# Banded attention followed by an MLP mixer: bfloat16 transposes, nine realigned score blocks, direct global columns and a bfloat16 bias pass

## The chip, the cores and the metric

The kernel runs on 1 core of one Trainium2 chip. The metric is the device time of one execution in microseconds (us), as the median of several executions. In this document PE is the TensorE matmul stream, PEld its weight loads, DVE VectorE, ACT ScalarE, POOL GpSimd and SP SyncE. "L306" means line 306 of the kernel that is being profiled, so a line number belongs to one kernel only.

## The reference

There are 8 batches of 8 heads, 576 positions, head size 64. Attention is limited to a band of ±32 positions, except that 8 "global" positions see everything and are seen by everything. Its output is the input of an MLP mixer (token mixing with a 576x576 matrix, then 512 → 2048 → 512 with ReLU).

```python
scores = scale * np.matmul(q, k.transpose(0, 1, 3, 2))      # scale = 1/8
mask = np.abs(pos[:, None] - pos[None, :]) <= 32
mask = mask | is_global[:, None] | is_global[None, :]
attn = softmax(np.where(mask, scores, -1e9))
x = (attn @ v) -> (batch, seq, 512)
a1 = alpha1 * x + beta1;  u = x + lam * einsum('ts,bsd->btd', w_tok, a1)
a2 = alpha2 * u + beta2;  out = u + lam * (np.maximum(a2 @ w_ch1, 0) @ w_ch2)   # float32
```

## The kernel before

There are three stages, and the profile shows them one after the other: setup (masks, weights in bfloat16, a bias vector), 64 attention heads, and the MLP. In these traces each engine runs its own instruction stream in a fixed order; the order within each engine is settled by a scheduler when the kernel is built, from the order in the source, the buffers and the dependences.

The bias pass of setup multiplies the raw float32 weights with `beta2`, one column at a time:

```python
W1[:, cc, :] = w1raw[:, cc, :] * a2c[:, cc]          # DVE, float32 -> bf16, 4 times (cut)
for ec in range(16):
    for cc in range(4):
        nc.tensor.matmul(out=bps[:, ec : ec + 1],
                         lhsT=w1raw[:, cc, ec * P : (ec + 1) * P],   # float32
                         rhs=b2c[:, cc : cc + 1], start=(cc == 0), stop=(cc == 3))
```

One head (cuts marked). `pA` has 2 buffers; the PSUM pools for the scores, the values (`pvps`) and the transposes (`trps`) have 1 each.

```python
BLOCKS = [(t, c) for t in range(5) for c in range(5) if abs(t - c) <= 1]   # 13 blocks

for h in range(H):
    dma_640(qn, qf, bh, nc.sync); dma_640(kn, kf, bh, nc.sync); dma_640(vn, vf, bh, nc.gpsimd)
    nc.scalar.copy(out=vext[:, :, 0:D], in_=vn)                    # ACT, to float16
    trps = psA_tr.tile([64, NT, P], FP32, name="trps")
    for c in range(NT):
        nc.tensor.transpose(out=trps[:, c, :], in_=qn[:, c, :], identity=ident)   # float32
    nc.vector.tensor_copy(out=QT, in_=trps)                        # DVE -> bf16
    for c in range(NT):
        nc.tensor.transpose(out=trps[:, c, :], in_=kn[:, c, :], identity=ident)   # same buffer
    nc.scalar.copy(out=KT, in_=trps)                               # ACT -> bf16

    nc.tensor.transpose(out=pvps[0:8, PV_VG:PV_VG+64], in_=vgT[:, 8*h:8*h+8], identity=...)
    nc.vector.tensor_copy(out=vg_ext[:, 0:D], in_=pvps[0:8, PV_VG:PV_VG+64])

    for bi, (t, c) in enumerate(BLOCKS):
        nc.tensor.matmul(out=scps[:, bi*P:(bi+1)*P], lhsT=KT[:, c, :], rhs=QT[:, t, :], ...)
        # ... where t == c: two products of 8 columns, for the global rows and global columns
    nc.scalar.activation(out=PT, in_=scps, func=AF.Exp, bias=0.0, scale=0.125)    # 1744 columns
    nc.vector.tensor_tensor(out=PT, in0=PT, in1=mask, op=ALU.mult)

    for t in range(NT):       # weights of the global columns, transposed on PE
        nc.tensor.transpose(out=pvps16[0:8, ...], in_=PT[:, GC_OFF+8*t : GC_OFF+8*t+8], identity=ident16)
    nc.vector.tensor_copy(out=pgcT, in_=pvps16[0:8, ...])
    for t in range(NT):       # values
        nc.tensor.matmul(out=pvps[:, t*65:t*65+65], lhsT=pgcT[:, t, :], rhs=vg_ext, ...)
        for c in neighbours(t):   # 13 in all
            nc.tensor.matmul(out=pvps[:, t*65:t*65+65], lhsT=PT[:, bi*P:(bi+1)*P], rhs=vext[:, c, :], ...)
    # ... 5 products for the global rows; then pvps -> xstg (DVE) and pvps -> xg (ACT)
```

The softmax here doesn't subtract the row's maximum and nothing guards it: scores larger than these inputs give would overflow.

## Time and profile before

The median is 1051.45 us (4 runs, 1050.48 to 1051.78). The profiled execution has a span of 1048.0 us. The stages are cut at the first score product and at the last copy into `xstg`:

| stage | us | what fills it |
|---|---|---|
| setup | 0 to 85.2 | DMA of weights, bias pass on PE, W2 on DVE, transposes of `w_tok` |
| 64 heads | 85.2 to 680.3 (595.1, or 9.30 a head) | PE |
| MLP | 680.3 to 1048.0 (367.7) | PE |

The windows view of before gives the busy time of each engine in each stage (in parentheses the number of instructions), then the granted clock, the busy share of the DMA engines and GB/s:

```profile
0.00:85.20 85.20, 41.05 (x177) 33.74 (x177) 28.93 (x86) 2.34 (x4) 7.83 (x14) 1.00 0.43 145
85.20:680.30 595.10, 500.61 (x3978) 324.07 (x3978) 200.82 (x531) 184.62 (x253) 89.03 (x151) 1.00 0.26 68
680.30:1048.00 367.70, 333.60 (x1987) 196.92 (x2024) 127.21 (x154) 127.17 (x257) 1.47 (x1) 1.00 0.17 59
```

The columns after the window's length are PE, PEld, DVE, ACT and POOL. In the heads PE is busy for 500.6 of 595.1 us, 84%; no other compute engine reaches 35%, and DMA stands at 0.26.

The chain of waits on before's page says what the end of the run followed from, here by engine (the page goes on by line):

```profile
PE 76%; DVE 9%; ACT 6%; DMA 5%; issue 2%; POOL 0%; SPq 0%; ACTq 0%; POOLq 0%; DVEq 0%
```

The same chain in order of time, over one head of before. Columns: start in us, duration in us, and what the chain passes through:

```profile
329.92 0.23 PE trps L291
...
330.17 0.83 DVE QT L292
331.00 0.04 issue
331.04 1.29 PE trps L294 x5
...
332.40 0.69 ACT KT L295
333.09 0.05 issue
333.14 0.28 PE scps L306
...
337.52 1.22 PE trps L291 x5
...
338.77 0.83 DVE QT L292
```

This is the pattern to see. There is one transpose buffer. PE transposes q into it (1.22 us), waits for DVE to copy it out (0.83 us), transposes k into it (1.29 us), and can do scores only when ACT has copied KT (0.69 us). From 331.04 to 339.64 (where the next k transposes start) is 8.6 us; many heads are longer, since the static order differs from head to head.

This is the timeline of before (columns: start, duration, engine, line and operation; in brackets the idle time of the engine before it and what ended it):

```profile
332.25 0.69 PE L327 MATMUL pvps<-ident,PT 128*8 128x128 f16 x5
333.14 0.28 PE L306 MATMUL scps<-QT,KT 64*128 64x128 bf16 x1 [0.20 <-ACT KT L295]
```

Over 530 us of heads (110 to 640 us) the two largest of PE's waits in the waits view are these (columns: total us, times, longest):

```profile
PE trps L294 <- DVE QT L292: 35.4, 43, 0.9
PE scps L306 <- ACT KT L295: 19.5, 43, 0.9
```

The groups view of before gives busy time and mean duration (ns) of the instructions that the change touches; after the second bar stands the idle time of the engine ahead of them and what ended it:

```profile
L294 PE MATMUL trps<-ident,kn 128*64 128x128 f32 x320 | 88.1, 421 | 54.3 <-DVE QT L292 38.8
L323 ACT ACTIVATE PT<-scps 128x1744 f16<-128x1744 f32 x64 | 103.9, 1624 | 77.6 <-PE scps L315 76.6
...
L295 ACT CAST KT<-trps 64x640 bf16<-64x640 f32 x64 | 43.8, 685 | 144.1 <-PE trps L294 129.8
...
L292 DVE CAST QT<-trps 64x640 bf16<-64x640 f32 x64 | 52.2, 815 | 53.3 <-PE trps L291 53.3
```

A transpose's record of 421 ns overlaps the next one's: five of them take 1.22 to 1.29 us in the chain, not 2.1.

The setup of before, again the chain in order of time:

```profile
16.56 13.12 DMA w1raw<-in_moe_w_ch_dram
...
29.81 27.45 PE bps L199 x128
...
57.46 9.62 DVE W L184 x16
```

The bias pass (its 64 float32 products stand in the trace as 128 passes, two each) takes 27.45 us on PE, and DVE's work on W2 comes after it.

### The profile page before, as it was taken

To read this page: it belongs to the slowest core of one execution; us is meant where nothing else is said; L and a number is where in the kernel's file an instruction comes from. 1 tells how busy PE (TensorE), PEld (TensorE's weight loads), DVE (VectorE), ACT (ScalarE), POOL (GpSimd) and SP (SyncE) were. 2 spreads that over 40 slices of the span, in tenths; PEclk is the share of its full clock that TensorE was granted. 3 is DMA by queue.
4 is the path that set the end of the run, shared out by engine and by line. 5 is a ranking of instruction groups with operands and counts; after the bars stand their busy time and mean duration, and the time that the engine had idled before them with its cause. 6 is when DMAs were issued, how large, how long until landed. Compare 5 with 4: busy or idle time off the path is not lost.

```text
span 1048.0 us, 14830 instructions
## 1 busy us (share of the span) xinstructions
PE 875.3 (84%) x6142; PEld 554.7 (53%) x6179; DVE 357.0 (34%) x770; ACT 314.1 (30%) x513; POOL 98.3 (9%) x165
## 2 busy tenths in 40 slices
PE   0857888888888888888888888629999999999988
PEld 0835555555555555555545555406565565565654
DVE  3152333333333233333333333345335144143021
ACT  0003233323333332333223333204152361441532
POOL 0004121111121011121111110000000000000000
PEclk9999999999999999999999999999999999999999
DMA  5603223223223132232232232041202112011001
GB/s 172 251 13 87 58 58 103 53 51 109 57 71 90 45 110 58 58 99 50 58 108 58 51 102 49 1 153 51 97 20 78 45 53 97 31 66 46 21 26 46
DMA packets 111291, 74.70 MB, mean 71 GB/s; under 512 B 89080, under 2 KB 89608, under 8 KB 110712
## 3 DMA queue, kind: packets, MB, share of 16 engines
q1 hardware_dynamic: 106088, 62.75, 20.3%
q0 software_dynamic: 5136, 11.00, 3.6%
q8 instruction: 49, 0.80, 0.3%
q14 instruction: 18, 0.15, 0.0%
HBM read 53.51 MB, written 20.22 MB: 70 GB/s over the span
## 4 chain that ended last, share of the span: by engine, by line
PE 76%; DVE 9%; ACT 6%; DMA 5%; issue 2%; POOL 0%; SPq 0%; ACTq 0%; POOLq 0%; DVEq 0%
PE chps L437 13%; PE hps L428 12%; PE scps L306 10%; PE pvps L340 8%; PE trps L294 7%; PE trps L291 7%; PE pvps L337 5%; DVE QT L292 4%; ACT KT L295 4%; PE tkps L403 3%; PE bps L199 3%; PE pvps L327 2%; PE pvps L348 2%; DMA X<-xdram 2%; PE utps L417 1%
## 5 line engine op out<-in xcount | busy, mean ns | idle before, releaser
L431 ACT ACTIVATE HT<-hps,bias1T 128x288 bf16<-128x288 f32 x256 | 127.0, 500 | 222.8 <-PE hps L428 222.8
L437 PE MATMUL chps<-W,HT 128*128 128x512 bf16 (+1 forms) x611 | 151.7, 380 | 0.8 <-issue 0.3
L428 PE MATMUL hps<-UT,W 128*128 128x288 bf16 x1024 | 147.4, 284 | 2.6 <-DVE UT L420 0.6
L306 PE MATMUL scps<-QT,KT 64*128 64x128 bf16 x832 | 123.9, 293 | 22.6 <-ACT KT L295 22.6
L294 PE MATMUL trps<-ident,kn 128*64 128x128 f32 x320 | 88.1, 421 | 54.3 <-DVE QT L292 38.8
L323 ACT ACTIVATE PT<-scps 128x1744 f16<-128x1744 f32 x64 | 103.9, 1624 | 77.6 <-PE scps L315 76.6
L428 PEld LDWEIGHTS <-W 128*128 128x128 bf16 x1024 | 98.9, 97 | 45.4 <-issue 21.2
L357 DVE COPY xstg<-pvps 128x320 f32<-128x320 f32 x64 | 31.4, 491 | 214.2 <-PE pvps L348 214.2
L340 PE MATMUL pvps<-vext,PT 128*128 128x65 f16 x832 | 103.5, 241 | 0.0
L441 DVE TENSOR_TENSOR ob<-chps,U 128x512 f32<-128x512 f32 (+1 forms) x40 | 27.6, 690 | 201.9 <-PE chps L437 175.7
L437 PEld LDWEIGHTS <-HT 128*128 128x128 bf16 (+1 forms) x640 | 62.2, 100 | 63.2 <-issue 3.4
L291 PE MATMUL trps<-ident,qn 128*64 128x128 f32 x320 | 89.7, 420 | 4.7 <-ACT KT L295 4.7
L294 PEld LDWEIGHTS trps<-ident,kn 128*64 128x64 f32 x320 | 42.5, 157 | 91.3 <-DVE QT L292 58.1
L306 PEld LDWEIGHTS <-KT 64*128 64x128 bf16 x832 | 66.3, 113 | 45.7 <-ACT KT L295 36.1
L295 ACT CAST KT<-trps 64x640 bf16<-64x640 f32 x64 | 43.8, 685 | 144.1 <-PE trps L294 129.8
L284 ACT CAST vext<-vn 128x320 f16<-128x320 f32 x64 | 29.3, 458 | 182.3 <-PE pvps L348 182.3
L337 PE MATMUL pvps<-vg_ext,pgcT 8*128 8x65 f16 x320 | 73.7, 230 | 0.6 <-DVE pgcT L333 0.6
L403 PE MATMUL tkps<-XL,wtT 128*128 128x512 bf16 (+2 forms) x192 | 52.0, 390 | 24.5 <-DVE XL L394 22.1
L292 DVE CAST QT<-trps 64x640 bf16<-64x640 f32 x64 | 52.2, 815 | 53.3 <-PE trps L291 53.3
L324 DVE TENSOR_TENSOR PT<-PT,mask 128x1744 f16<-128x1744 f16 x64 | 67.2, 1050 | 3.6 <-ACT PT L323 3.6
L308 PE MATMUL scps<-qgT,KT 64*128 64x8 bf16 x320 | 67.3, 210 | 0.0
L340 PEld LDWEIGHTS <-PT 128*128 128x128 f16 x832 | 52.8, 116 | 20.6
(82 smaller groups left out, 813.4 us busy)
## 6 DMA issues: line engine op xcount, KB each, us to landing
xdram<-xstg SPq DMA_DIRECT2D x8, 1300.0 KB, 6.4
X<-xdram SPq DMA_DIRECT2D x8, 1300.0 KB, 5.9
qn<-in_q_dram SPq DMA_DIRECT2D x63, 160.0 KB, 2.7
kn<-in_k_dram SPq DMA_DIRECT2D x63, 160.0 KB, 2.4
vn<-in_v_dram POOLq DMA_DIRECT2D x63, 160.0 KB, 3.2
out_dram<-ob SPq DMA_DIRECT2D x32, 256.0 KB, 2.0
w1raw<-in_moe_w_ch_dram SPq DMA_DIRECT2D x1, 4096.0 KB, 13.1
w2raw<-in_moe_w_ch_dram SPq DMA_DIRECT2D x1, 4096.0 KB
```

The source lines that it names most:

```text
L291: nc.tensor.transpose(out=trps[:, c, :], in_=qn[:, c, :], identity=ident)
L292: nc.vector.tensor_copy(out=QT, in_=trps)
L294: nc.tensor.transpose(out=trps[:, c, :], in_=kn[:, c, :], identity=ident)
L295: nc.scalar.copy(out=KT, in_=trps)
L306: nc.tensor.matmul(out=scps[:, bi * P : (bi + 1) * P], lhsT=KT[:, c, :], rhs=QT[:, t, :], start=True, stop=True)
L323: nc.scalar.activation(out=PT, in_=scps, func=AF.Exp, bias=0.0, scale=0.125)
L337: nc.tensor.matmul(out=pvps[:, t * PV_T : t * PV_T + PV_T], lhsT=pgcT[:, t, :], rhs=vg_ext, start=True, stop=False)
L340: nc.tensor.matmul(out=pvps[:, t * PV_T : t * PV_T + PV_T], lhsT=PT[:, bi * P : (bi + 1) * P], rhs=vext[:, c, :], start=False, stop=(ci == ...
L403: nc.tensor.matmul(out=tkps[0:tsz, :], lhsT=wtT[0:ssz, sc, t * P : t * P + tsz], rhs=XL[0:ssz, sc, :], start=(sc == 0), stop=(sc == 4),)
L428: nc.tensor.matmul(out=hps, lhsT=W1[:, cc, ec * P : (ec + 1) * P], rhs=UT[:, cc, tsl], start=(cc == 0), stop=(cc == 3))
L431: nc.scalar.activation(out=HT[:, ec, tsl], in_=hps, func=AF.Relu, bias=bias1T[:, ec : ec + 1], scale=1.0)
L437: nc.tensor.matmul(out=chps[0:tsz, :], lhsT=HT[:, ec, t * P : t * P + tsz], rhs=W2[:, ec, :], start=(ec == 0), stop=(ec == 15))
```

## The change

The intent is to shorten every head on PE and to shorten setup:

- q and k are first cast to bfloat16 (qn on DVE, kn on ACT), and the transposes and their PSUM tile are bfloat16. KT is copied by DVE instead of ACT.
- The 13 score blocks of 128x128 become 9. A tile of 128 queries needs only the keys from 32 before to 32 after it, which fit into two blocks of 128 if these start at an odd multiple of 64 (the first tile keeps its blocks at 0 and 128, the last needs only one). That needs a second load of v, shifted by 64 rows (`vo`, `voext`).
- The weights of the global columns are computed with the global keys as the stationary operand, so they come out already transposed: two products into an own PSUM tile `gcps` and an own exp, in place of five 8-column products, five transposes and a copy.
- The global v rows are transposed once a batch, not once a head. `pvps` gets two buffers.
- The bias pass uses the bfloat16 W1, with beta2/alpha2 as the moving operand.

```diff
-BLOCKS = [(t, c) for t in range(NT) for c in range(NT) if abs(t - c) <= 1]
+BLOCKS = [(0, 0), (0, 128), (1, 64), (1, 192), (2, 192), (2, 320), (3, 320), (3, 448), (4, 448)]
 # ... (tables of the mask for the new blocks cut)
+    nc.vector.reciprocal(out=ra2c, in_=a2c)
+    nc.vector.tensor_tensor(out=b2a, in0=b2c, in1=ra2c, op=ALU.mult)      # bf16
-                    lhsT=w1raw[:, cc, ec * P : (ec + 1) * P],
-                    rhs=b2c[:, cc : cc + 1],
+                    lhsT=W1[:, cc, ec * P : (ec + 1) * P],
+                    rhs=b2a[:, cc : cc + 1],
 # ...
-        tc.tile_pool(name="psA_pv", bufs=1, ...) as psA_pv,
+        tc.tile_pool(name="psA_pv", bufs=2, ...) as psA_pv,
+        tc.tile_pool(name="psA_gc", bufs=1, ...) as psA_gc,
 # ... once a batch:
+            for h in range(H):
+                nc.tensor.transpose(out=vgps[:, 64*h : 64*h+64], in_=vgT[:, 8*h : 8*h+8], identity=...)
+            nc.vector.tensor_copy(out=vg_all[:, :, 0:D], in_=vgps...)
 # ... once a head:
+                nc.vector.tensor_copy(out=qn16, in_=qn)
+                nc.scalar.copy(out=kn16, in_=kn)
+                nc.gpsimd.dma_start(out=vo, in_=vf[bh * S + 64 : bh * S + S, :]...)
+                nc.scalar.copy(out=voext[:, :, 0:D], in_=vo)
-                trps = psA_tr.tile([64, NT, P], FP32, name="trps")
+                trps = psA_tr.tile([64, NT, P], BF16, name="trps")
-                    nc.tensor.transpose(out=trps[:, c, :], in_=qn[:, c, :], identity=ident)
+                    nc.tensor.transpose(out=trps[:, c, :], in_=qn16[:, c, :], identity=identb)
-                nc.scalar.copy(out=KT, in_=trps)
+                nc.vector.tensor_copy(out=KT, in_=trps)
-                        # five: lhsT=QT[:, t, :], rhs=kgT[:, 8*h : 8*h+8]
+                nc.tensor.matmul(out=gcps[0:8, PV_GCB:PV_GCB+128], lhsT=kgT[:, 8*h:8*h+8], rhs=QT[:, 4, :], ...)
+                nc.tensor.matmul(out=gcps[0:8, 512:1024], lhsT=kgT[:, 8*h:8*h+8], rhs=QTf[:, 0:512], ...)
+                nc.scalar.activation(out=pgc, in_=gcps[0:8, PV_GCB:1024], func=AF.Exp, ...)
-                # five transposes of PT's global columns, copy to pgcT
```

## The prediction

> **What bounds it now** (chain of waits, timeline). Setup runs to about 84 us; 64 attention heads from 84 to 680 us (first score matmul to last copy into xstg, 9.31 us a head); the MLP takes 368 us. The chain of waits is 76% PE. From 330 to 347 us (two heads) PE issues about 7.7 us a head: float32 transposes of q and k 1.22 and 1.29 (five each), scores 1.9, five transposes of the global-column weights 0.62, the value products 2.47, one vg transpose 0.2. About 1.6 us a head is PE waiting for the two copies out of the one transpose buffer (QT on DVE 0.82, KT on ACT 0.69).
>
> **What the change does, per head.**
> - Float32 transposes become bfloat16. Five 16-bit transposes of PT take 0.69 us start to end in the trace, 0.62 occupied. Saves about 1.3 us of PE.
> - QT reads 16-bit PSUM. The copy of pgcT (640 16-bit elements from PSUM) takes 0.48 us against 0.82 for 640 float32; the Trainium skill, "VectorE: DVE Perf Modes", section "Why PSUM operands drop a tier", gives the same factor. KT moves to DVE, also 0.48.
> - Score blocks 13 to 9, and five 8-column products become two products of 640 columns: about 1.9 to 1.65 us.
> - Five pgcT transposes and the pgcT copy vanish; value products 2.47 to about 2.05 (at 0.06-0.07 us each).
> - Exp 1744 to 1192 columns: 1.62 to 1.16 us (0.85 ns a column in the trace); mask product 1.05 to 0.77.
> - Added: casts of qn (DVE, 0.25, from the W1 cast) and kn (ACT 0.46), voext (ACT 0.40), exp of pgc (ACT 0.7), a second value load (POOL 0.9, 128 KB).
>
> Sums per head: PE 5.0, ACT 3.4, DVE 2.7, POOL 2.0 us; DMA busy share from 0.27 to about 0.57.
>
> **The new loop.** PE's static order in a head is: scores, one global product, q transposes, k transposes, global-column products, value products. With DVE in the order QT, qn cast, mask: scores end at 1.28, q transposes 2.15, QT 2.66, qn cast 2.83, mask 3.5; meanwhile k transposes and the global products end at 3.65; value products end at 5.6. The period is about 5.65 us, perhaps 6 with slips. At each batch border vg_all is copied from the score buffer before the next scores: about 0.9 us, seven times.
>
> Attention: 64 x 5.75 + 6 + filling, about 380 us against 596: 216 saved.
>
> **Setup.** The 128 float32 passes for bias1T (27.4 us on PE, holding DVE) become 64 bfloat16 ones, about 5 us after W1. Then W2 (copied from 57.4 us on) waits for its DMA, done near 42 us by the DMA share in windows. About 15 us saved; DVE's longer mask setup (4-5 us) fits before w1raw lands at 29.8 us. The MLP is unchanged.
>
> **Time: 1051 - 216 - 15 = 820 us, range 785 to 870.** Faster by over 2%: 0.97; within 2%: 0.02; slower: 0.01.
>
> **Right if** the stage of heads spans about 380 us, PE is the largest part of its chain, q/k transposes cost about 0.1 us each, bias1T ends near 40 us, the MLP still takes 368 us. **Wrong if** DVE's in-order queue (mask behind QT and the qn cast, KT behind the mask) or ACT (vext and voext casts ahead of exp) makes PE wait over 1 us a head; if value loads on POOL arrive late; if these transposes cost more than those of PT.

## The result, and the profile after

The median after is 828.49 us (8 runs, 826.57 to 829.34); before took 1051.07 us in the same rounds (12 runs). The ratio is 0.788 (95% interval 0.7869 to 0.7888). Ratios here are the mean time of one kernel's runs over that of the other's of the same rounds, so they are not quite the ratio of the medians quoted.

| stage | before | after | saved | predicted |
|---|---|---|---|---|
| setup | 85.2 | 69.0 | 16.2 | 15 |
| heads | 595.1 | 388.1 | 207.0 | 216 |
| MLP | 367.7 | 368.7 | −1.0 | 0 |

The windows view of after, with the same columns (the last 0.7 us of the span are cut off):

```profile
0.00:69.00 69.00, 16.34 (x123) 8.99 (x124) 33.39 (x111) 3.91 (x7) 9.44 (x21) 1.00 0.54 184
69.00:457.00 388.00, 357.08 (x2945) 236.67 (x2945) 163.76 (x474) 198.22 (x377) 146.42 (x282) 1.00 0.49 125
457.00:825.00 368.00, 334.57 (x1987) 197.38 (x2024) 127.31 (x155) 127.28 (x257) 1.47 (x1) 1.00 0.17 59
```

In the heads PE's busy time fell by 143.5 us, from 500.6 to 357.1; the rest of the 207 us saved, about 64 us, is time in which PE had not been busy (94.5 us before, 30.9 after). ACT and POOL are busier than before, DMA share nearly doubled, and neither holds PE up.

The chain of waits on after's page:

```profile
PE 79%; DMA 9%; DVE 8%; issue 2%; ACT 1%; SPq 0%; POOL 0%; POOLq 0%; DVEq 0%
```

ACT has left the chain in the heads (6% before, 1% after): KT is no longer waited for. The chain in order of time over one head of after:

```profile
299.42 0.22 PE scps L341
...
300.76 0.69 PE trps L325 x5
301.45 0.02 issue
301.47 0.49 DVE QT L326
301.97 0.04 issue
302.01 0.69 PE trps L328 x5
302.70 0.20 PE gcps L353
302.90 0.43 PE gcps L354
303.33 0.22 PE pvps L369 x2
...
305.04 0.37 PE pvps L378 x5
305.41 0.22 PE scps L341
```

A head is now 5.99 us (299.42 to 305.41), it repeats regularly except at the batch borders, and one wait is left in it: PE waits for QT, 0.57 us by the timeline. The wait for KT is filled, because PE does the global-column products and the value products meanwhile. Over 340 us of heads the waits view, for PE alone, has this one line (columns: total us, times, longest):

```profile
PE trps L328 <- DVE QT L326: 24.1, 42, 0.6
```

The groups of after that answer to those shown of before:

```profile
L357 ACT ACTIVATE PT<-scps 128x1192 f16<-128x1192 f32 x64 | 74.5, 1165 | 37.7 <-PE scps L346 37.7
...
L328 PE MATMUL trps<-identb,kn 128*64 128x128 bf16 x320 | 46.6, 307 | 27.5 <-DVE QT L326 27.0
L326 DVE COPY QT<-trps 64x640 bf16<-64x640 bf16 x64 | 30.9, 483 | 89.2 <-PE trps L325 89.2
...
L360 ACT ACTIVATE pgc<-gcps 8x640 f16<-8x640 f32 x64 | 44.4, 693 | 23.1 <-PE gcps L354 21.3
```

Setup of after, the chain in order of time:

```profile
17.16 23.17 DMA w2raw<-in_moe_w_ch_dram
40.35 9.72 DVE W L202 x16
50.07 0.68 DVE wtT L236
```

The bias pass is gone from the chain. DVE now starts on W2 at 40.35 us, when the DMA of W2 lands (it was predicted for 42), and this DMA has become the limit of that part of setup.

### The profile page after: what moved, and what is told of

Its sections match the earlier page's. It is cut to its first block, busy times and chain, and to the rows that moved or that the text cites. A ratio compares the mean times of both kernels' runs of the same rounds, so it can differ in the third digit from the quotient of the medians.

```text
span 825.7 us, 13171 instructions
## 1 busy us (share of the span) xinstructions
PE 708.0 (86%) x5054; PEld 443.0 (54%) x5091; DVE 324.5 (39%) x737; ACT 329.4 (40%) x641; POOL 157.3 (19%) x303
## 4 chain that ended last, share of the span: by engine, by line
PE 79%; DMA 9%; DVE 8%; issue 2%; ACT 1%; SPq 0%; POOL 0%; POOLq 0%; DVEq 0%
PE chps L465 16%; PE hps L456 15%; PE scps L341 9%; PE pvps L369 8%; PE pvps L364 6%; PE trps L325 5%; PE trps L328 5%; PE tkps L433 3%; DMA X<-xdram 3%; PE gcps L354 3%; PE pvps L378 3%; DVE QT L326 3%; DMA w2raw<-in_moe_w_ch_dram 3%; DMA g_rep<-in_global_idx_dram 2%; PE utps L447 1%
## 5 line engine op out<-in xcount | busy, mean ns | idle before, releaser
L465 PEld LDWEIGHTS <-HT 128*128 128x128 bf16 (+1 forms) x640 | 62.2, 100 | 63.4 <-issue 3.4
L357 ACT ACTIVATE PT<-scps 128x1192 f16<-128x1192 f32 x64 | 74.5, 1165 | 37.7 <-PE scps L346 37.7
L341 PE MATMUL scps<-QT,KT 64*128 64x128 bf16 x576 | 79.7, 288 | 0.6 <-DVE KT L329 0.6
L364 PE MATMUL pvps<-vg_all,pgc 8*128 8x65 f16 x320 | 74.1, 232 | 0.0
L369 PE MATMUL pvps<-voext,PT 128*128 128x65 f16 x448 | 71.1, 240 | 0.0
L328 PE MATMUL trps<-identb,kn 128*64 128x128 bf16 x320 | 46.6, 307 | 27.5 <-DVE QT L326 27.0
L326 DVE COPY QT<-trps 64x640 bf16<-64x640 bf16 x64 | 30.9, 483 | 89.2 <-PE trps L325 89.2
L265 POOL DMA_DIRECT2D vn<-in_v_dram x63 | 54.9, 872 | 26.0 <-ACT vext L313 20.6
L328 PEld LDWEIGHTS <-kn 128*64 128x64 bf16 x320 | 38.2, 165 | 36.9 <-issue 35.3
L360 ACT ACTIVATE pgc<-gcps 8x640 f16<-8x640 f32 x64 | 44.4, 693 | 23.1 <-PE gcps L354 21.3
L316 POOL DMA_DIRECT2D vo<-in_v_dram x64 | 50.4, 788 | 4.2 <-ACT vext L313 2.1
```

Source lines behind the costliest of these rows:

```text
L265: eng.dma_start(out=dst, in_=src_flat[bh * S : bh * S + SPAD, :].rearrange("(c p) d -> p c d", p=P))
L328: nc.tensor.transpose(out=trps[:, c, :], in_=kn16[:, c, :], identity=identb)
L341: nc.tensor.matmul(out=scps[:, bi * P : (bi + 1) * P], lhsT=KTf[:, c : c + P], rhs=QT[:, t, :], start=True, stop=True)
L357: nc.scalar.activation(out=PT, in_=scps[:, 0:SCORE_F], func=AF.Exp, bias=0.0, scale=0.125)
L364: nc.tensor.matmul(out=pvps[:, t * PV_T : t * PV_T + PV_T], lhsT=pgc[:, gsl], rhs=vg_ext, start=True, stop=False)
L369: nc.tensor.matmul(out=pvps[:, t * PV_T : t * PV_T + PV_T], lhsT=PT[:, bi * P : (bi + 1) * P], rhs=rhs, start=False, stop=(ci == len(tbis) ...
```

## Experiments

The theory: the heads are limited by the work that PE issues in its fixed order plus its waits for the single transpose buffer, and the change shortens both. The rivals: the gain comes from the PSUM copies alone (QT and KT in 16 bits, or KT on another engine); from the second `pvps` buffer; or from less exp, mask and score work off PE.

There are two kinds of experiment: one part of the change put into before alone, and one part taken out of after. The kernels ran in four groups, each group beside before on one chip; before's medians there were 1051.4 to 1054.5 us. Where a kernel is set against after, the quotient of the two ratios to before is used. The outputs are right.

| run | what | median us | ratio to before |
|---|---|---|---|
| e1_bias_only | before + bf16 bias pass | 1039.35 | 0.986 |
| e2_tr16_only | before + bf16 casts and transposes, KT on ACT | 989.69 | 0.939 |
| e2b_tr16_f32psum | e2, but the PSUM tile stays float32 | 1013.99 | 0.962 |
| e3_blocks_only | before + nine blocks | 985.44 | 0.935 |
| e2c_tr16_kt_dve | e2 with KT on DVE | 1014.99 | 0.962 |
| e2d_tr16_vgall | e2 + global v rows once a batch | 966.06 | 0.918 |
| e4_gc_transposed | after, global columns transposed as in before | 877.95 | 0.832 |
| e6_pv1 | after, one `pvps` buffer | 831.96 | 0.789 |
| e7_tr32_pv1 | e6 with float32 transposes, no casts | 921.04 | 0.874 |
| e8_kt_act | after, KT copied by ACT | 849.26 | 0.805 |
| g1_joint_tr | after, q and k transposed together | 806.41 | 0.765 |
| g2_pipelined | g1, heads pipelined in the source | 766.28 | 0.727 |

### Parts of the change alone, put into before

**e1_bias_only.** Only the bias pass is changed.

```diff
-                    lhsT=w1raw[:, cc, ec * P : (ec + 1) * P],
-                    rhs=b2c[:, cc : cc + 1],
+                    lhsT=W1[:, cc, ec * P : (ec + 1) * P],
+                    rhs=b2a[:, cc : cc + 1],
```

> The kernel before with the bias vector alone in bfloat16. Theory: setup shortens until W2's DMA (landed at 40.3 us in the changed kernel) holds the DVE, so 16 us are saved, about 1035 us; heads and MLP as before. Rival: the bias pass was wholly on the chain, so its saving is 27.4 minus about 5, 22 us or more: about 1029 us or less. Second rival: setup is bound by loads alone: 1051.

Measured: 1039.35 us against 1053.14, 14 us less. The first score product starts at 68.6 us instead of 85.2, and in the chain the DMA of W2 ends at 40.7 us with DVE's work on W2 right behind it:

```profile
16.93 23.77 DMA w2raw<-in_moe_w_ch_dram
...
40.72 9.72 DVE W L189 x16
```

The theory holds for setup, which is 16.6 us shorter; in the profiled run the heads and the MLP came out 2.6 and 1.2 us longer. Of the 22 us that PE no longer spends, the DMA of W2 gives back some.

**e2_tr16_only.** Casts, bfloat16 transposes, bfloat16 PSUM; KT stays on ACT, everything else is before.

```diff
+                nc.vector.tensor_copy(out=qn16, in_=qn)
+                nc.scalar.copy(out=kn16, in_=kn)
-                trps = psA_tr.tile([64, NT, P], FP32, name="trps")
+                trps = psA_tr.tile([64, NT, P], BF16, name="trps")
-                    nc.tensor.transpose(out=trps[:, c, :], in_=qn[:, c, :], identity=ident)
+                    nc.tensor.transpose(out=trps[:, c, :], in_=qn16[:, c, :], identity=identb)
```

> The kernel before with q and k cast to bfloat16 and transposed in bfloat16 (PSUM in bfloat16), nothing else. Theory (PE issue bounds the heads, and the waits for the one transpose buffer come on top): per head 1.22+1.29 becomes 2 x 0.69 on PE, 1.13 saved, and QT 0.82 becomes 0.48, 0.34 saved; together 1.47 x 64 = 94 us, about 957 us. Rival (only the copies out of PSUM count, PE has slack): 0.34 x 64 = 22 us, about 1029 us.

Measured: 989.69 against 1053.14, 63 us less: far more than the rival (copies alone) allows, and 30 us short of the theory's sum. The trace shows where these went. From 150 to 600 us PE now waits 36.6 us for DVE to free the single `pvps` buffer (its last reader is the small copy of xg's denominators, L368), 22.2 us for KT, and 15.5 us for vg_ext. The removed PE work turned in part into new waits in DVE's and ACT's queues.

**e2b_tr16_f32psum.** The same, but the transposes are written as products with the identity into a float32 PSUM tile, so PE is cheap and the copies stay expensive.

```diff
-                trps = psA_tr.tile([64, NT, P], BF16, name="trps")
+                trps = psA_tr.tile([64, NT, P], FP32, name="trps")
-                    nc.tensor.transpose(out=trps[:, c, :], in_=qn16[:, c, :], identity=identb)
+                    nc.tensor.matmul(out=trps[:, c, :], lhsT=qn16[:, c, :], rhs=identb, start=True, stop=True)
```

> As the run with bfloat16 transposes alone, but as plain products with the identity into float32 PSUM, so the copies out stay at 0.82 and 0.69 us. Theory: the PE share alone is saved, 1.13 x 64 = 72 us, about 979 us; 22 us slower than with bfloat16 PSUM. Rival (copies count, not PE): about 1051 us.

Measured: 1013.99, 24 us slower than e2. The size is that of the copies' share (22 expected), but the run doesn't show it to be this share, since the waits are others than in e2: PE's waits for KT grow from 22.2 to 98.1 us, and those for xg (36.6) go. Against before it saved 39 us, not 72. The reason can be read from two views. First PE's waits from 150 to 600 us in e2b:

```profile
PE scps L313 <- ACT KT L302: 98.1, 45, 2.5
```

Then its timeline at one of these waits:

```profile
401.08 1.62 ACT L330 ACTIVATE PT<-scps 128x1744 f16<-128x1744 f32 x1
...
402.69 0.68 ACT L302 CAST KT<-trps 64x640 bf16<-64x640 f32 x1
...
403.42 0.28 PE L313 MATMUL scps<-QT,KT 64*128 64x128 bf16 x1 [2.20 <-ACT KT L302]
```

KT's copy takes 0.68 us, but PE waits 2.20 us for it. KT is on the same engine as exp, ACT runs its instructions in the built order, and exp (1.62 us) stands in front of it: KT starts at 402.69, when exp ends. A faster PE reaches its wait earlier and then waits for exp. How much it waits depends on the built order: e2 has the same PE work and 22.2 us of this wait.

**e3_blocks_only.** The nine blocks, `vo` and `voext` go into before; the transposes stay float32, the global columns as they were.

```diff
-BLOCKS = [(t, c) for t in range(NT) for c in range(NT) if abs(t - c) <= 1]
+BLOCKS = [(0, 0), (0, 128), (1, 64), (1, 192), (2, 192), (2, 320), (3, 320), (3, 448), (4, 448)]
+                nc.gpsimd.dma_start(out=vo, in_=vf[bh * S + 64 : bh * S + S, :]...)
+                nc.scalar.copy(out=voext[:, :, 0:D], in_=vo)
```

> The kernel before with the 9 realigned blocks in place of 13 (and the second value load), all else as before. Theory: PE saves four score products (about 0.1 each) and four value products (0.07 each), 0.68 x 64 = 44 us, about 1007 us; the shorter exp (1.62 to about 1.2) and mask product (1.05 to 0.78) are hidden under PE. Rival: exp and mask lie on the chain of each head, so 0.42 and 0.27 come on top, 1.37 x 64 = 88 us, about 963 us. Second rival: the added load on POOL and cast on ACT cost more than the blocks give: 1051 us or slower.

Measured: 985.44, 68 us less, where the theory's sum said 44; the rival (88) is not it either. PE's waits from 150 to 600 us in e3 hold no line for KT:

```profile
PE trps L316 <- DVE QT L314: 43.6, 48, 0.9
PE pvps L355 <- DVE vg_ext L324: 14.5, 48, 0.3
```

In e3 the heads follow one another regularly, 8.26 us apart, and the static order puts the vg transpose and the five transposes of PT (0.69 us in the chain) between the k transposes and the scores, so KT is copied while PE works. The extra gain of 24 us fits the waits for KT that this order covers (19.5 us of PE's waits in 530 us of before's heads); it is a by-product of the schedule, not of the blocks as such.

**e2c_tr16_kt_dve.** KT of e2 moves to DVE, to take it from behind exp.

```diff
-                nc.scalar.copy(out=KT, in_=trps)
+                nc.vector.tensor_copy(out=KT, in_=trps)
```

> The kernel before with 16-bit transposes alone gained 63 us, where 94 were expected; its trace shows PE waiting for KT (queued on ACT behind exp) and for a copy of xg behind the same exp. Here KT is copied by DVE as well. Theory (the in-order queue of ACT behind the 1.62 us exp eats the saving of PE): the waits for KT, 22 us in 450 us of that trace, go: 28 us, about 962 us; the wait for xg stays. Rival (16-bit transposes just save less than their durations say): no change, 990.

Measured: 1014.99, 25 us slower than e2. Both the theory (962) and the rival (990) fall. PE's waits from 150 to 600 us in e2c:

```profile
PE scps L313 <- ACT PT L330: 62.2, 46, 1.5
```

With KT on DVE the scheduler put the next scores right after the k transposes, and PE then waits for exp to have read the only score buffer. In after the same copy on DVE is worth a gain (e8 below). A part's worth depends on the order that it is built into.

**e2d_tr16_vgall.** e2 with the global v rows transposed once a batch, which removes one transpose, one copy and one user of `pvps` a head.

```diff
-                nc.tensor.transpose(out=pvps[0:8, PV_VG : PV_VG + 64], in_=vgT[:, 8 * h : 8 * h + 8], ...)
-                nc.vector.tensor_copy(out=vg_ext[:, 0:D], in_=pvps[0:8, PV_VG : PV_VG + 64])
+                vg_ext = vg_all[:, h, :]
```

> The kernel before with 16-bit transposes and one more part of the change: the vg rows are transposed once a batch, not once a head into the value bank. With 16-bit transposes alone PE waited 36.6 us for a copy of xg before the vg transpose and 15.5 us for a copy of vg, in 450 us of that trace. Theory (the missing 30 us of the 94 lay in these two waits): 52 x 9.3/8.3 or about 55 us go, less 10 us for the work at the batch borders, about 945 us (930 to 960). Rival (the waits move elsewhere, since another static order comes out): 975 to 990.

Measured: 966.06, 22 us less than e2 by the medians' distance to before (85.3 against 63.4 us); the theory's range (930 to 960) is missed narrowly, the rival's (975 to 990) too. The waits moved on again (34.8 us for DVE's xg copy, now before the transposes of PT, 28.5 us for KT). So the vg wait was a part of what e2 lacked, and not the whole.

Together: the bias pass, the transposes and the blocks, each alone, gained 14, 63 and 68 us, 145 in sum; the whole change gained 223. The remainder is not in any one of these parts. Part of it is the direct global columns, which the next section measures.

### Parts taken out of after

**e4_gc_transposed.** In after, the global columns are again five 8-column products, a longer exp, five transposes and a copy.

```diff
-                nc.tensor.matmul(out=gcps[0:8, PV_GCB : PV_GCB + 128], lhsT=kgT[...], rhs=QT[:, 4, :], ...)
-                nc.tensor.matmul(out=gcps[0:8, 512:1024], lhsT=kgT[...], rhs=QTf[:, 0:512], ...)
+                for t in range(NT):
+                    nc.tensor.matmul(out=scps[:, SCORE_F+8*t : SCORE_F+8*t+8], lhsT=QT[:, t, :], rhs=kgT[...], ...)
+                # ... after exp and mask:
+                    nc.tensor.transpose(out=gcps[0:8, t*P:(t+1)*P], in_=PT[:, SCORE_F+8*t:SCORE_F+8*t+8], identity=ident16)
+                nc.vector.tensor_copy(out=pgc, in_=gcps[0:8, 0:SPAD])
-                nc.scalar.activation(out=pgc, in_=gcps[0:8, PV_GCB:1024], func=AF.Exp, bias=0.0, scale=0.125)
```

> The changed kernel with one part undone: the global columns again as five 8-column products in the score buffer, exp with the rest, five 16-bit transposes and a copy of pgcT on DVE. Theory (PE issue plus what PE must wait for in order): PE 0.2 more for the five products, 0.62 for the transposes, 0.63 less for the two long products, and the value products now wait for exp, transposes and the copy (0.48 us) in turn: 0.75 us a head, 48 us, about 876 us. Rival (only the count of PE work): 0.2 x 64 = 13 us, about 841 us.

Measured: 877.95; 0.8322/0.7879 = 1.056, so 47 us slower than after. The theory's 876 holds, the rival's 841 falls. PE's waits from 100 to 440 us show a wait that after doesn't have, for the copy that is back on the path:

```profile
PE pvps L377 <- DVE pgc L373: 21.8, 38, 0.6
```

**e6_pv1.** One `pvps` buffer in after.

```diff
-        tc.tile_pool(name="psA_pv", bufs=2, ...) as psA_pv,
+        tc.tile_pool(name="psA_pv", bufs=1, ...) as psA_pv,
```

> The changed kernel with one buffer for the value products in place of two. Its static order stays the same but for the first global product of a head, which moves behind the global-column products. Theory (the second buffer only lets that one product go early): 0.16 us a head or less, about 838 us at most. Rival (the gain of the change is mostly overlap from double buffering, not less PE work): +100 us or more.

Measured: 831.96; 0.7894/0.7879 = 1.002. The second buffer is worth about 2 us at most, which the intervals (0.7873 to 0.7915 against 0.7869 to 0.7888) do not tell from nothing, and the rival (+100) falls: in after's timeline PE spends about 4 us on scores, transposes and global columns between the last value product of one head and most of those of the next, and DVE empties `pvps` meanwhile.

**e7_tr32_pv1.** e6 with float32 transposes and without the casts (it has one `pvps` buffer, as e6 has, so it is read against e6).

```diff
-                nc.vector.tensor_copy(out=qn16, in_=qn)
-                nc.scalar.copy(out=kn16, in_=kn)
-                trps = psA_tr.tile([64, NT, P], BF16, name="trps")
+                trps = psA_tr.tile([64, NT, P], FP32, name="trps")
-                    nc.tensor.transpose(out=trps[:, c, :], in_=qn16[:, c, :], identity=identb)
+                    nc.tensor.transpose(out=trps[:, c, :], in_=qn[:, c, :], identity=ident)
```

> The changed kernel with float32 transposes (no casts of q and k; one buffer for the value products[...], so it is to be read against the run with one such buffer, 832 us). Theory: PE 1.13 us more a head, QT and KT 0.34 longer each, of which one is waited for: 1.47 x 64 = 94 us, about 926 us. Rival (the parts overlap each other as they did when added alone to the kernel before, where 16-bit transposes gave 63): about 895 us.

Measured: 921.04, 89 us more than e6; 926 was expected, and the rival's 895 falls. This is the sum of durations: ten transposes at about twice the price, and two copies of 0.82 instead of 0.48 us of which one is waited for in most heads.

**e8_kt_act.** KT is copied by ACT in after.

```diff
-                nc.vector.tensor_copy(out=KT, in_=trps)
+                nc.scalar.copy(out=KT, in_=trps)
```

> The changed kernel with KT copied by ACT, as before the change. Theory: with the long exp gone and the order scores, q, k, global products, values, KT (0.69 on ACT behind exp) ends near 3.7 us of a head and is needed at 6, so no change: within 8 us of 828. Rival (moving KT off the engine of exp carries the gain, as in the kernel before with 16-bit transposes alone, where PE waits up to 2.5 us for a KT queued behind exp): +1 us a head, 64 us, about 892.

Measured: 849.26; 0.805/0.7879 = 1.022, 18 us slower. That is more than the theory's 8 and far less than the rival's 64. PE waits only 6.6 us for KT from 100 to 440 us. The scheduler built another order, in which PE starts two or three of the next head's scores before the values in about half of the heads; heads of about 6.0 and 6.4 us alternate. So KT's engine is worth 18 us with the order that comes with it, but the main gain doesn't come from it. The theory missed this because it took the order to stay.

### Further versions that the experiments pointed to

**g1_joint_tr.** QT is the one wait left, and each of the ten transposes fills only half of the array (the groups view gives their stationary operand as 128*64). So q and k are cast side by side into one tile of 128 columns, and five transposes do both.

```diff
+                qk16 = pA.tile([P, NT, 2 * D], BF16, name="qk16")
+                nc.vector.tensor_copy(out=qk16[:, :, 0:D], in_=qn)
+                nc.scalar.copy(out=qk16[:, :, D : 2 * D], in_=kn)
-                trps = psA_tr.tile([64, NT, P], BF16, name="trps")
+                trps = psA_tr.tile([P, NT, P], BF16, name="trps")
+                    nc.tensor.transpose(out=trps[:, c, :], in_=qk16[:, c, :], identity=identb)
+                nc.vector.tensor_copy(out=QT, in_=trps[0:D])
+                nc.vector.tensor_copy(out=KT, in_=trps[D:P])
```

> Not a part of the change: q and k of a chunk side by side, so that five transposes of 128 columns take the place of ten of 64, and QT and KT are copied from the two halves. Theory (PE still bounds the changed kernel, with 0.57 us a head of waiting for QT between the two sets): 0.69 of PE and part of the wait go, until the run of scores, exp, mask and values (about 5.3 us) binds: about 0.5 us a head, 795 us (785 to 808). Rival (DVE's and ACT's in-order queues bound it): no gain, 828 or slower.

Measured: 806.41; 0.7652/0.7879 = 0.971, 24 us less than after, inside the expected range, at its slow end (795 was its middle). PE's waits from 100 to 440 us put 20.2 us on DVE's small xg instruction ahead of the values. By the timeline at one of them, exp had ended at 258.72 us, but the mask product that the values read started only at 260.22, behind the copy into `xstg` in DVE's queue, and xg's instruction came right after it. DVE's order has become the wait.

**g2_pipelined.** The source order is changed so that a head's scores, the next head's loads and transposes, and the previous head's values follow each other; `pA` gets 3 buffers. Nothing else differs from g1.

```diff
+        for bh in range(NH):
+            scores(bh)
+            if bh + 1 < NH:
+                loads(bh + 1)          # loads, casts, transposes, QT, KT
+            # ... (next batch's global rows cut)
+            if bh > 0:
+                values(bh - 1)
+        values(NH - 1)
```

> Not a part of the change: joint transposes, and the source written so that the scores of a head come before the values of the head in front of it (three buffers in place of two). Theory (with joint transposes PE has 4.7 us of work a head and waits for exp, mask and copies that are in order behind work for another head): PE is fed from another head while exp and mask run, 4.8 to 5.3 us a head, 750 to 785 us. Rival (the static order that the scheduler makes, or DVE and ACT, bind): no better than the joint transposes alone, 806 us.

Measured: 766.28 us (764.79 to 767.44), ratio to before 0.7273; 0.7273/0.7879 = 0.923, so 7.7% faster than after. It beats both kernels. The windows view of g2 over 230 us of heads:

```profile
150.00:380.00 230.00, 221.25 (x1871) 141.62 (x1868) 127.89 (x341) 133.91 (x271) 102.74 (x203) 1.00 0.65 155
```

PE is busy for 221.25 of 230 us, 96%, where after has 93% there (213.94 us); the other engines carry more per us and still don't hold it up.

## Why the prediction was right, and where a term was off

The predicted 820 us (785 to 870) against 828.5 measured is right in direction, size and mechanism: PE sets the pace of the heads, and the change takes work and waits from it. Point by point:

- **Heads.** "about 380 us against 596" became 388.1 us against 595.1. That PE's issue work and waits for the transpose buffer set the pace is borne out by the experiments that undo a part: e4 and e7 cost what their durations sum to (47 and 89 us), and e6 nothing much. The sums a head were less exact: by the windows view, divided by 64, PE is busy for 5.6 us in after (5.0 predicted) and was for 7.8 in before (7.7), ACT for 3.1 (3.4), DVE for 2.6 (2.7), POOL for 2.3 (2.0). So PE's work fell by 143.5 us where the prediction's sums say 173.
- **Waits before.** The prediction put the wait for the two copies at about 1.6 us a head, the sum of the copies' durations. That is too much: 64 times 1.6 is 102 us, and PE is idle for only 94.5 us in all of before's heads. In the waits view KT costs PE 19.5 us ahead of the scores in 530 us, about 0.34 us a head and not 0.69, because PE often has other work meanwhile. The time that PE sat idle still fell by 64 us, 1.0 us a head.
- **Transposes.** Five took 0.69 us, as predicted from those of PT in before. e7 shows the worth of these transposes and their copies within the new loop: 89 us.
- **Copies.** QT fell from 815 to 483 ns. The Trainium skill, "VectorE: DVE Perf Modes", section "Why PSUM operands drop a tier", says that a PSUM operand limits a copy to the two-fold mode and float32 to the one-fold; the trace agrees in kind, with a factor of 1.7 (815 to 483 ns) rather than 2; no run separates what keeps it from 2.
- **Exp.** 1624 ns became 1165 (1.16 predicted). The Trainium skill, "ScalarE: Activation LUTs", section "What ACT_TABLE_LOAD costs", gives 186 ns + 0.833 ns a column for immediate scale and bias, hence estimates of 1639 and 1179 ns; both agree to 1.5%.
- **Static order.** PE's order in a head came out as predicted: scores, one global product, q transposes, k transposes, global-column products, values. Up to QT the times fit (counted from 299.35 us, where the timeline has the first score product start): scores end 1.25 us after the head's start (1.28 predicted), QT is copied at 2.61 (2.66).
- **Setup.** 16.2 us saved, 15 predicted, with the DMA of W2 as the new limit. e1 shows the bias pass alone does it. In before its 128 passes start 0.213 us apart, in after the 64 bfloat16 ones (L217) 0.027 us.
- **MLP.** 368.7 us, not changed.

**The term that was mis-sized** is this step: "meanwhile k transposes and the global products end at 3.65". From QT at 2.66 to 3.65 are 0.99 us, of which the transposes take 0.69; about 0.30 us was left for the two global-column products. They took 0.20 + 0.43 = 0.63 us in the chain of after, and ended at 3.98 instead of 3.65. With that, 5.65 becomes 5.98, and 5.99 was measured. Over 64 heads 0.33 us are 21 us. The prediction had added 0.1 us a head of reserve (5.75), 6 us in all, and 12 us for borders and filling, of which about 5 were needed (388.1 less 64 x 5.99). So the reserve and, by luck, the cheap borders covered part of the miss, and the heads ended 8 us late.

Why they cost double can be read from the trace: in streams of 128 columns during the heads, and of 512 at the start of the MLP, the array passes one column in about 0.83 ns (1/1.2), half as fast as in most of the MLP (0.216 us for 512 columns, 0.42 ns each). The timeline of after shows the same product (128x512, bfloat16) five times among the first products of the MLP, and five times 3 us later:

```profile
479.16 2.34 PE L433 MATMUL tkps<-XL,wtT 128*128 128x512 bf16 x5 [0.22 <-issue]
...
482.55 1.24 PE L433 MATMUL tkps<-XL,wtT 128*128 128x512 bf16 x5 [0.29 <-DVE U L440]
```

By the single starts in the trace they lie 0.427 us apart up to 481.3 us and 0.216 us apart from 481.7 on; the trace's first clock record of this run begins at 481.6 us and says full rate. The global-column product of 512 columns (L354) has a record of 630 ns throughout the heads, like the first kind (634) and unlike the second (377). The bfloat16 transposes of 128 columns lie 0.107 us apart in the heads, which is 128/1.2. The Trainium skill, "TensorE: Matmul & The Clock Gate", section "Back-to-back issue gap", gives for a product of N columns by itself, from start to start, N/1.2 ns for its cold state and N/2.4 + 2.5 ns for its warm one (its words for the half and the full clock rate): 427 and 216 ns for 512 columns. The spacings in this trace agree with both to the nanosecond; by them the heads are at the cold rate and the MLP, from 481.7 us on, at the warm one. It is the same in before (the first clock record at 705.8 us, in the MLP too). So the prediction's durations that were read from the heads of before were right, and the one that had no counterpart there was taken at too fast a rate. (That the prediction took the MLP's rate is an inference: 640 columns at 0.42 ns are 0.27 us, close to the 0.30 it left; at 0.83 ns they are 0.53. The remaining 0.1 us of the 0.63 isn't columns.)

Smaller misses: qn's cast took 0.32 us, not 0.25; e8 and e2c show that the choice of DVE or ACT for KT was less simple than in the prediction, since it changes the built order.

What stays open: which rule makes the scheduler build which order, and hence why parts put into before alone gain other amounts than their durations say (63 instead of 94 for the transposes, 68 instead of 44 for the blocks) is shown only by the resulting waits. Whether the shorter exp and mask product pay by themselves wasn't measured: no run makes only them longer. Nor was the nine-block part taken out of after: what the runs on after and e1 account for (47, 89, 18 and 14 us) leaves about 55 of the 223 us to the blocks and to the global v rows together, by subtraction and not by experiment. And what keeps the array at half rate in the heads is not tested.

## What to carry to other kernels

If one engine issues nearly all the time in a regular loop, sums of its durations taken from the trace predict what a removed or added instruction costs within a few us, as long as the built order stays (e4, e6, e7; in e8 it didn't, and 18 us came where none were expected); in a loop with waits they don't, because the saved time runs into the next wait in an in-order queue (e2, e2b) and the built order changes. Take the rate of a product from a product of the same stage, start to start, and not from another stage or from its record's length. Take a wait from the waits view and not from the duration of what is waited for. Once PE's work is cut, look at the source order of the loop: pipelining the heads brought 40 us more (806 to 766) without removing any work.

## What the Trainium skill lacked or had wrong

- "TensorE: Matmul & The Clock Gate", Part 1, section "What's actually happening", has the array warm after one sustained busy window of about 3.4 us. Here it stayed at the cold spacing through 388 us of heads in after, and in g2 through 230 us with PE busy for 96% by its records (transposes of 128 columns 0.107 us apart, the 512-column product's record 630 ns). "Part 4: PE-mode transpose" of the same page says that transposes do not count as busy in the same way; a head has ten of them in after and five in g2, and no run here takes them out, so whether they are the reason stays open.
- The same page, section "Seeing it yourself", warns that single clock events of a trace can't be fully trusted, but not that they can be missing for most of a run: the granted clock reads 1.00 for all stages of before and after, because the trace has no clock record before 481.6 us (705.8 in before). Only the spacings show the half rate.
- The same page, "Part 4: PE-mode transpose", gives 275 to 390 ns for one transpose but no spacing in a stream: 0.107 us for bfloat16 and 0.214 us for float32 in the heads, and 0.109 us for float32 in the MLP.
- "FP8 and Floating Point Precision", section "TensorE Precision Notes", gives four passes for true float32. It has no figure for transposes: float32 ones cost twice the bfloat16 ones here (0.214 against 0.107 us in the heads of before and of after), not four times.
- "TensorEngine Tiling (Array Packing)" has no figure for what it costs, in a stream of short products, to go from a stationary operand of one shape to one of another. In the chain of before one product with 8 rows (L337) and two with 128 rows (L340), of 65 columns each, take 0.16 + 0.22 = 0.38 us, and with three of 128 rows 0.16 + 0.28 = 0.44. So one more product of 128 rows adds 0.06 us, and the one of 8 rows, with the changes to it and back, costs about 0.26. No run separates the product from the changes.
- "ScalarE: Activation LUTs", section "What ACT_TABLE_LOAD costs", gives 1283 ns for the load and about 1380 ns of drain after it. The trace of before has the load with just 1283 ns at 82.8 us, and the copy behind it starts at 84.1 us, so no drain was visible there. It is the only load of the run, so no switch from one table to another was seen.
